# RetNet and SwiGLU in one kernel: the first pair of heads by chunks of 128 tokens behind identity products, and another order of the first loads

## The chip, the cores and the metric

The kernel runs on one core of a Trainium2 chip. The metric is device time in microseconds; lower is better. Before the change three runs took 1016.43, 1018.75 and 1019.09 us (median 1018.75). A profiled execution took 1014.55 us.

## What is computed

A retention layer feeds a gated feed-forward block. q, k and v are (8, 8, 576, 64) in float32: 8 sequences, 8 heads, 576 tokens, 64 channels.

```python
gamma = 1.0 - 2.0 ** (-5.0 - np.arange(H))                     # one decay per head
Dmat = np.where(rel >= 0, gamma[:, None, None] ** rel, 0.0)    # rel = i - j
ret = (scale * q @ k.T) * Dmat
x = (ret @ v).transpose(0, 2, 1, 3).reshape(4608, 512)
g = x @ w_gate                                                 # (512, 1536)
out = (g * sigmoid(g) * (x @ w_val)) @ w_out                   # (1536, 512)
```

The three weights arrive as float64 and are turned into float32 on the chip.

## The kernel before

**Pairs.** Two heads lie side by side on the 128 partitions and are called a pair; there are 32 of them, four per sequence. Retention is done by chunks of tokens: inside a chunk, scores times decay times v ("own values"); from earlier chunks, a running state of 64 x 64 per head ("earlier values"). Chunks have 64 tokens. For each pair, `transposes` (L448) turns k and q by products with the identity `ident` and copies them out of PSUM, `scores` (L562) makes the products of k and q, `new_states` (L537) those of k and v, `masked` (L576) multiplies scores by the decay and runs the states forward on DVE, `own_values` (L524) and `earlier_values` (L546) add up the outputs in the PSUM tile `outer`, and `to_x` (L613) copies them to the x of the next stage. Keys are scaled on ACT, DVE or, for pairs 2 and 3, on POOL (L505); for pairs 1 to 3 of the first sequence, q is scaled by position on POOL (`scale_run`, L730).

**Feed-forward.** The first 512 tokens go through plain products: `up0(f, chunks)` (L842) multiplies x by gate and value columns f of 12, where "chunks" are pairs 0 to 3 as the four pieces of the contraction. `up0(f)` writes gate and value into bankA and bankB for even f, bankC and bankE for odd f, and ends with SiLU on ACT (L856) and a product on DVE (L857). The later tokens go through tiles of 1024 with sums of operands; that part is the bulk of the run and the change leaves it alone.

**Weights.** A block of weights is 1 MB of float64. `load_w(m)` (L359) asks for the m-th block, `split(j)` (L380) takes the j-th half block apart with two ACT operations (L389, L390), `rounding(j)` (L399) puts it together with two on DVE (L406, L407) and, if `ahead` is set, calls the next `split`. Blocks 0 and 1 are gate and value of `up0(0)` and `up0(1)`, 2 and 3 of `up0(2)` and `up0(3)`, 4 and 5 of the next two. There are three landing places; block 3 has one of its own in `x_odd`. A place is free when its split is done, and `split` then asks for the next block.

**Order.** The order on each engine is the order in which the Python code issues instructions. Before, a loop over `tick(t, 0, HP)` (L737) runs the first four pairs as a pipeline: at step t, scores and states of pair t-1, own values of pair t-2, transposes of pair t, earlier values of pair t-2. Weights are first needed at step 4, when `up0(0, range(2))` (L757) is issued. Then `up0` for pieces 2 and 3 follows, and a written plan of `up0`, `rounding` and later ticks.

**Loads.** DMAs of SyncE (SP) and of ACT go out in program order, and each uses one of eight landing semaphores in turn: an issue waits until the DMA eight before has landed. SP asks for the small table (64 columns, L311), pairs 0 to 2, the big table (512 columns, L337), pair 3, the first halves of blocks 0 and 1 in pieces of 256 KB, their second halves, blocks 2 and 3 in four pieces each, pair 4 (`load(HP)`) and block 4. ACT shares the loads of pairs 0 and 1 and asks for the blocks from 5 on.

Of the kernel before, what the change touches and what calls it, by code (L numbers as in the profile page):

```python
# [22 lines left out]
def tables(gamma, scale, L):  # L23

    g, at = np.array(gamma), np.arange(L)
    lane = np.arange(2 * L)[:, None]
    both = lambda t: np.repeat(t, L, axis=0).reshape(-1, 2 * L, t.shape[1]).transpose(1, 0, 2).reshape(2 * L, -1)
    twice = lambda t: np.concatenate([t, t])
    half = [np.repeat(g.reshape(-1, 2), L, axis=1).T ** (lane % 32 + 32 * r) for r in range(2)]
    pieces = scale * np.stack(half, axis=2).reshape(2 * L, -1)
    runs = scale * (g[None, :, None] ** ((4 * lane[:, :, None] + np.arange(4)) % L)).reshape(2 * L, -1)
    parts = [twice((g[:, None] ** -at).T), twice((g[:, None] ** (L - at)).T),
             both(g[:, None] ** L), both(g[:, None] ** (2 * L)), pieces, runs, both(scale * g[:, None] ** at),
             both((scale * g[:, None] ** at).reshape(-1, 2, L)[:, ::-1].reshape(-1, L))]  # L40
    return np.concatenate(parts, axis=1).astype(np.float32)
# [90 lines left out]
def kernel(  # L132
# [32 lines left out]
    nc = tc.nc  # L165
# [88 lines left out]
    def load(i):  # L254
# [6 lines left out]
        if i < HP:  # L261
# [11 lines left out]
            for h in heads:  # L273
                queues[i % 2].dma_start(out=blocks(t)[:, h % 2], in_=v[b, h, 0:CW].rearrange("(c p) d -> p c d", p=P))
# [35 lines left out]
    NCOL = 6 * H + 4 * HP  # L310
    nc.sync.dma_start(out=tab[:, 0:NCOL], in_=decays[:, 0:NCOL])  # L311
    load(0)
    load(1)
    ident = const.tile([P, P], F32, name="ident")
    make_identity(nc, ident)
    nc.scalar.activation(out=io[:, 0:1], in_=ident[:, 0:1], func=AF.Silu)
    inv, key = tab[:, 0:H], tab[:, H : 2 * H]
    step = tab[:, 2 * H : 2 * H + 2 * HP]
    piece = tab[:, 2 * H + 2 * HP : 2 * H + 4 * HP]
    run = tab[:, 2 * H + 4 * HP : NCOL]  # L320
# [11 lines left out]
    even_heads, odd_heads = slice(0, H, 2), slice(1, H, 2)  # L332
    for rows in half:
        decay(slice(0, H), slice(0, H), rows)

    load(2)
    nc.sync.dma_start(out=tab[:, NCOL:], in_=decays[:, NCOL:])  # L337
    load(3)
# [20 lines left out]
    def load_w(m, parts=range(2)):  # L359

        i, queue = order[m], nc.sync if m < 5 else nc.scalar
        n = m - (m > RAWS)
        raw = rest[:, raw_at + n % RAWS * 2048 : raw_at + (n % RAWS + 1) * 2048].rearrange("p (c x) -> p c x", c=HP)
        if m == RAWS:
            raw = x_odd[:, :, TW // 2 :]
        raws[i] = raw.bitcast(I32)
        dst, src = raw.bitcast(I64), weights[i][0]
        if i < NUP:
            for cols in [ts(2 * f + n, D) for f in parts for n in range(2)] if m <= RAWS else [slice(0, 2 * P)]:
                queue.dma_start(out=dst[:, :, cols], in_=src[:, :, cols])  # L370
        else:
            queue.dma_start(out=dst.rearrange("p (f c) n -> p f (c n)", f=2), in_=src)
# [38 lines left out]
    for f in range(2):  # L411
        for m in range(2):
            load_w(m, (f,))
# [30 lines left out]
    def vector(i):  # L444

        return i == 0

    def transposes(i):  # L448
# [6 lines left out]
        copy = nc.scalar.copy if i else nc.vector.tensor_copy  # L455
        if i < HP:

            mine = (bankC, bankE) if i + 1 == HP else (bankB, bankA)
            parts = [(kT, kn, mine[0]), (qT, qk, mine[1])]
            if i == 0:  # L460
                parts.reverse()

            def turn(t, src, bank):
                for c in range(NFULL):
                    to = bank[:, c : 4 * P : NFULL] if t is qT and scaled(i) else bank[:, ts(c, P)]
                    nc.tensor.transpose(to, src[:, ts(c, P)], ident)

            def put(t, _, bank):
                if i or t is qT:
                    copy(t[:, 0:CW], bank)  # L470
                else:
                    copy(t[:, 0 : CW // 2], bank[:, 0 : CW // 2])
                    nc.scalar.copy(t[:, CW // 2 : CW], bank[:, CW // 2 :])

            if i + 1 == HP:
                for part in parts:
                    turn(*part)
                pieces = [lambda part=part: put(*part) for part in parts]
            else:
                for part in parts:  # L480
                    turn(*part)
                    put(*part)
# [13 lines left out]
        def keys():  # L496
# [5 lines left out]
            for hl, rows, at in parts:  # L502
                scale = key[rows, 2 * p + hl : 2 * p + hl + 1]
                if vector(i) or 1 < i < HP:
                    (nc.vector if vector(i) else nc.gpsimd).tensor_scalar(out=at, in0=at, scalar1=scale, scalar2=None, op0=ALU.mult)  # L505
                else:
                    nc.scalar.activation(out=at, in_=at, func=AF.Copy, scale=scale)
# [3 lines left out]
        return [keys] + pieces  # L511
# [64 lines left out]
    def masked(i):  # L576
# [6 lines left out]
        def copies():  # L583
            (nc.vector.tensor_copy if vector(i + 1) else nc.scalar.copy)(out=even, in_=z[:, 0])
# [151 lines left out]

    def tick(t, lo=HP, hi=NP, spread=False, then=None):  # L737
        go_on(len(pieces))
        if hi == HP:

            def new_pair():
                scores(t - 1, True)
                new_states(t - 1)
                pieces.extend(masked(t - 1))
                go_on(3)

            scale_run(t + 1)
            if lo < t < hi:
                new_pair()
            if lo <= t - 2 < hi:  # L750
                own_values(t - 2)
            for f in transposes(t) if lo <= t < hi and t + 1 < HP else ():
                f()
            if lo <= t - 2 < hi:
                earlier_values(t - 2)
                if t == HP:
                    up0(0, range(2))  # L757
                to_x(t - 2)[0]()
            if t + 1 == HP:
                split(0)  # L760
                after = transposes(t)
                rounding(0)
                for f in after:
                    f()
            if t == HP:
                rounding(2)
                rounding(3, False)
                new_pair()
                while held:
                    held.pop()()  # L770
                split(4)
                up0(1, range(2))
            return
# [68 lines left out]
    def up0(f, chunks):  # L842

        pair = banks[2 * (f % 2) : 2 * (f % 2) + 2]
        for gv, bank in enumerate(pair):
# [581 lines left out]
    for t in range(HP + 2):  # L1427
        tick(t, 0, HP)

        if t == 3:  # L1430
            load(HP)
        for j in {3: (1,), 5: (4, 5)}.get(t, ()):
            rounding(j)
    for c in range(2, HP):
        for f in range(2):
            up0(f, [c])
    load(HP + 1)
# [20 lines left out]
    plan.insert(1, lambda: tick(HP, HP, FIRST))  # L1458
    tick_at = {2: 4, 3: 5, 5: 6, 7: 7, 10: 8, 11: 9}
    for f in range(2, NF):  # L1460
        round_until({4: 12, 6: 13, 8: 14, 9: 15, 10: 16, 11: 17}.get(f, f + 2))
# [108 lines left out]
```

## Time and profile before

| | us |
|---|---|
| profiled execution | 1014.55 |
| its span on the core | 1012.8 |
| PE busy | 1000.9 |
| DVE busy | 710.9 |
| POOL busy | 561.8 |
| ACT busy | 286.7 |
| first transposes on PE (L466) | at 4.63 |
| first product with a weight (L853) | at 24.11 |
| first product of `up0(2)` (L850) | at 40.95 |

The span is the time between the first and the last instruction of the core in the profile; 1.75 us of the execution lie around it. A busy time is the union of the engine's instructions, and a matmul's record holds some 0.2 us of its passage through the array, so that neighbours overlap; the distance from start to start tells the rate. A float32 product is two passes, and counts in the profile ("x32") are passes; a transpose is one. A line of the timeline holds start, length, engine, line, operation, output <- inputs, partitions x elements, and the count; in brackets stand the idle time ahead and what ended it.

### The profile page before, as it was taken

What the parts mean: (1) busy time and instruction counts of PE and PEld (TensorE: products, weight loads), DVE (VectorE), ACT (ScalarE), POOL (GpSimd) and SP (SyncE); (2) the same over time, 40 slices, a digit from 0 to 9 for tenths busy, and PEclk for the clock granted to TensorE, in tenths of its full rate; (3) what the DMA queues carried; (4) which work ended last, traced back from release to release, by engine and by line L of the source; (5) the groups of instructions that cost most, each with busy time, mean ns of one, the idle gap of its engine ahead of it and who ended that gap; (6) DMA issues with size and microseconds to landing.
All of it is one profiled execution on the core that took longest, in us unless ns stands there. A gap on an engine that the chain in (4) does not pass through costs nothing.

```text
span 1012.8 us, 21319 instructions
## 1 busy us (share of the span) xinstructions
PE 1000.9 (99%) x8336; PEld 825.5 (82%) x8336; DVE 710.9 (70%) x1206; ACT 286.7 (28%) x636; POOL 561.8 (55%) x589
## 2 busy tenths in 40 slices
PE   6999999999999999999999999999999999999998
PEld 5655555888888888888888888888888888888887
DVE  4488887677875766977777678866575767566645
ACT  4565522132423312133422202233220012232110
POOL 3400359979375228575564157746672586566514
PEclk9999999999999999999999999999999999999999
DMA  9999866967587787647677777434454554445553
GB/s 245 261 288 272 192 216 234 264 193 214 138 238 207 217 231 193 198 156 196 184 202 206 198 179 217 154 133 159 161 172 141 154 189 147 148 155 180 182 159 102
DMA packets 278892, 194.38 MB, mean 192 GB/s; under 512 B 212552, under 2 KB 246088, under 8 KB 278792
## 3 DMA queue, kind: packets, MB, share of 16 engines
q1 hardware_dynamic: 251464, 94.70, 36.7%
q10 hardware_dynamic: 26688, 97.92, 29.1%
q8 instruction: 66, 1.08, 0.5%
q0 software_dynamic: 640, 0.39, 0.2%
q14 instruction: 34, 0.28, 0.1%
HBM read 154.04 MB, written 38.93 MB: 191 GB/s over the span
## 4 chain that ended last, share of the span: by engine, by line
PE 94%; DVE 2%; DMA 1%; POOL 1%; SPq 0%; issue 0%; ACT 0%; DVEq 0%; ACTq 0%; POOLq 0%
PE bankB L1186 12%; PE bankC L1186 11%; PE bankA L1186 11%; PE bankE L1186 11%; PE bankB L1392 7%; PE bankC L1392 7%; PE bankE L1392 6%; PE bankA L1392 6%; PE outer L532 2%; PE bankE L853 2%; PE bankA L853 2%; PE outer L1186 2%; PE inner L1186 2%; PE bankB L853 2%; PE outer L559 2%; PE bankC L853 2%
## 5 line engine op out<-in xcount | busy, mean ns | idle before, releaser
L1042 POOL TENSOR_TENSOR rest<-rest 128x512 f32<-128x512 f32 (+1 forms) x139 | 148.0, 1076 | 159.9 <-DVE rest L1042 112.5
L1201 POOL TENSOR_TENSOR arena<-rest,io 128x256 f32<-128x256 f32 x168 | 123.9, 750 | 89.4 <-ACT io L1200 88.9
L1200 ACT ACTIVATE io<-rest 128x256 f32<-128x256 f32 x192 | 79.3, 417 | 200.0 <-DVE rest L1042 140.0
L1186 PE MATMUL bankB<-rest,arena 128*128 128x256 f32 x448 | 114.5, 380 | 0.0
L1042 DVE TENSOR_TENSOR rest<-bankB,rest 128x512 f32<-128x512 f32 x116 | 78.5, 685 | 40.5 <-PE bankB L1186 28.5
L1186 PE MATMUL bankC<-rest,arena 128*128 128x256 f32 x416 | 106.3, 380 | 0.0
L1186 PE MATMUL bankA<-rest,arena 128*128 128x256 f32 x412 | 104.8, 379 | 0.0
L1042 DVE TENSOR_TENSOR rest<-bankA,rest 128x512 f32<-128x512 f32 x111 | 75.2, 685 | 40.8 <-PE bankA L1186 19.3
L1042 DVE TENSOR_TENSOR rest<-bankC,rest 128x512 f32<-128x512 f32 x110 | 74.5, 683 | 38.0 <-PE bankC L1186 23.4
L1042 DVE TENSOR_TENSOR rest<-bankE,rest 128x512 f32<-128x512 f32 x106 | 71.7, 684 | 36.2 <-PE bankE L1186 17.6
L1186 PE MATMUL bankE<-rest,arena 128*128 128x256 f32 x372 | 94.9, 380 | 0.3 <-DVE rest L1042 0.3
L1186 PEld LDWEIGHTS bankB<-rest,arena 128*128 128x128 f32 x448 | 84.7, 190 | 11.9 <-DVE rest L1042 0.2
L1186 PEld LDWEIGHTS bankC<-rest,arena 128*128 128x128 f32 x416 | 78.5, 190 | 11.4 <-DVE rest L1042 0.8
L1186 PEld LDWEIGHTS bankA<-rest,arena 128*128 128x128 f32 x412 | 78.1, 190 | 10.9 <-DVE rest L1042 0.2
L1186 PEld LDWEIGHTS bankE<-rest,arena 128*128 128x128 f32 x372 | 70.3, 190 | 10.4 <-DVE rest L1042 0.8
L1042 POOL TENSOR_TENSOR arena<-arena 128x256 f32<-128x256 f32 (+1 forms) x76 | 70.3, 947 | 11.1 <-PE bankC L1186 9.0
L886 POOL TENSOR_TENSOR rest<-rest 128x512 f32<-128x512 f32 x21 | 28.5, 1377 | 72.1 <-DVE rest L407 58.5
L1392 PE MATMUL bankB<-arena 128*128 128x256 f32 x264 | 61.0, 381 | 0.0
L1392 PE MATMUL bankE<-arena 128*128 128x256 f32 x264 | 60.8, 380 | 0.0
L1392 PEld LDWEIGHTS bankE<-arena 128*128 128x128 f32 x264 | 50.0, 190 | 6.9
L1392 PEld LDWEIGHTS bankB<-arena 128*128 128x128 f32 x264 | 49.8, 190 | 6.9
L1392 PE MATMUL bankC<-arena 128*128 128x256 f32 x240 | 55.2, 379 | 0.0
(270 smaller groups left out, 1876.0 us busy)
## 6 DMA issues: line engine op xcount, KB each, us to landing
arena<-up ACTq DMA_DIRECT2D x63, 896.0 KB, 4.6
arena<-dn ACTq DMA_DIRECT2D x65, 384.0 KB, 3.1
arena<-dn SPq DMA_DIRECT2D x39, 384.0 KB, 3.1
out_dram<-rest SPq DMA_DIRECT2D x31, 256.0 KB, 3.4
qk<-in_q_dram SPq DMA_DIRECT2D x108, 72.0 KB, 3.1
qk<-in_k_dram SPq DMA_DIRECT2D x108, 72.0 KB, 3.4
dn<-rest SPq DMA_DIRECT2D x26, 256.0 KB, 2.8
up<-arena SPq DMA_DIRECT2D x13, 512.0 KB, 5.6
```

What stands on the lines that cost most here:

```text
L532: m = nc.tensor.matmul(value(i, hl, c), s["v"][rows, at], ret[rows, c % 2 if whole(i) else hl, c // 2], start=start, stop=start, skip_grou ...
L559: nc.tensor.matmul(xr[half[hl]] if c + 1 == NC else value(i, hl, c), state[half[hl], c, :], s["qT"][half[hl], ts(c, L)], start=False, stop ...
L853: nc.tensor.matmul(bank, w, xs[0][:, c, :], start=(c == 0), stop=(c == HP - 1))
L886: eng.tensor_tensor(out=dst, in0=srcs[0], in1=srcs[1], op=ALU.add if op[0] == "add" else ALU.subtract)
L1042: eng.tensor_tensor(out=out, in0=a, in1=b, op=ALU.add if sign > 0 else ALU.subtract)
L1186: m = nc.tensor.matmul(b[:, g * TB : (g + 1) * TB], w[:, g], x, start=(opens and g == 0), stop=True, skip_group_check=True)
L1200: nc.scalar.activation(out=s, in_=src[:, 0:TB], func=AF.Silu)
L1201: (nc.vector if busy and o != 2 and qd + 1 < NQ else nc.gpsimd).tensor_tensor(out=hid[:, qd, 2 * H + h, 2 * T + t], in0=src[:, TB : 2 * TB ...
L1392: nc.tensor.matmul(b[:, m * TB : (m + 1) * TB], lhs[:, qd, ts(m, P)], w[:, qd], start=(opens and qd == 0 and m == 0), stop=(qd == NQ - 1), ...
```

## The change

It has four parts.

1. **Pair 0 by chunks of 128 tokens.** `first_scores`, `first_states`, `first_own` and `first_out` replace the general functions for pair 0: 8 products of 128 x 128 for scores instead of 16 of 64 x 64, 8 for the states, 8 for own values, 6 for earlier ones. q is scaled where it is copied out of PSUM, so the output is a plain ACT copy. Three small tables (4 + 128 columns) are added to the first table.
2. **Identity products.** `first_scores` begins with two 64 x 64 and six 128 x 128 products of the identity with itself, and has two and one more behind the transposes of q and k. Six small ones also stand ahead of the first up product.
3. **The order of the first stage is written out.** The first product of `up0(0)` now stands behind own values of pair 1, and the further ones between the work of pairs 1 to 3.
4. **Loads.** SP asks for q and k of pair 0 first, then the table. The values of a pair are a step of their own (`values`). The first halves of blocks 0 and 1 come ahead of pair 3, their second halves behind it; blocks 2 and 3 are one DMA each. Block 4 now stands ahead of pair 4, the big table behind it. Block 5 is asked for on ACT behind the outputs of pair 3 (`held`), and `split(6)` behind `up0` of all four pieces. `tick(HP, HP, FIRST)` moves from ahead of `up0(2)` to behind it.

```diff
-    NCOL = 6 * H + 4 * HP
-    nc.sync.dma_start(out=tab[:, 0:NCOL], in_=decays[:, 0:NCOL])
-    load(0)
-    load(1)
+    NCOL = 6 * H + 4 * HP + 4 + P
+    values = [load(0), load(1)]
     ident = const.tile([P, P], F32, name="ident")
     make_identity(nc, ident)
     nc.scalar.activation(out=io[:, 0:1], in_=ident[:, 0:1], func=AF.Silu)
+    for f in values:
+        f()
+    load(2)()
...
-    load(2)
-    nc.sync.dma_start(out=tab[:, NCOL:], in_=decays[:, NCOL:])
-    load(3)
...
-            for cols in [ts(2 * f + n, D) for f in parts for n in range(2)] if m <= RAWS else [slice(0, 2 * P)]:
+            for cols in [ts(2 * f + n, D) for f in parts for n in range(2)] if m < 2 else [slice(0, 2 * P)]:
...
-    for f in range(2):
-        for m in range(2):
-            load_w(m, (f,))
+    for m in range(2):
+        load_w(m, (0,))
+    load(3)()
+    for m in range(2):
+        load_w(m, (1,))
     load_w(2)
     load_w(3)
...
+    def first_scores():
...
+        for _ in range(2):
+            nc.tensor.matmul(bankB[0:D, 0:D], ident[0:D, 0:D], ident[0:D, 0:D], start=True, stop=True)
+        for src, bank, idle in ((None, None, 6), (qk, bankE, 2), (kn, bankC, 1)):
+            for c in range(NFULL if bank else 0):
+                nc.tensor.transpose(bank[:, ts(c, P)], src[:, ts(c, P)], ident)
+            for _ in range(idle):
+                nc.tensor.matmul(bankB[:, 0:P], ident, ident, start=True, stop=True)
...
+        nc.vector.tensor_tensor(out=blocks(qT), in0=blocks(bankE), in1=table(first_qry), op=ALU.mult)
+        nc.vector.tensor_copy(kT[:, 0 : CW // 2], bankC[:, 0 : CW // 2])
+        nc.scalar.copy(kT[:, CW // 2 : CW], bankC[:, CW // 2 :])
+        for hl in range(2):
+            at = kn[:, 0:CW].rearrange("p (g d) -> p g d", d=D)[:, hl::2]
+            nc.vector.tensor_scalar(out=at, in0=at, scalar1=first_key[:, hl : hl + 1], scalar2=None, op0=ALU.mult)
+        for c, hl in first:
+            nc.tensor.matmul(inner[:, hl, ts(c, P)], kT[half[hl], ts(c, P)], qT[half[hl], ts(c, P)],
+                             start=True, stop=True, skip_group_check=True)
+        for hl in range(2):
+            nc.vector.tensor_tensor(out=first_ret[:, hl], in0=blocks(inner[:, hl]), in1=table(first_near[:, ts(hl, P)]), op=ALU.mult)
+
+    def first_states():
...
+    def first_own():
...
+    def first_out():
...
-    for t in range(HP + 2):
-        tick(t, 0, HP)
-
-        if t == 3:
-            load(HP)
-        for j in {3: (1,), 5: (4, 5)}.get(t, ()):
-            rounding(j)
+    scale_run(1)
+    first_scores()
+    scale_run(2)
+    turn_pair(1)
+    first_states()
+    first_own()
+    new_pair(1)
+    turn_pair(2)
+    first_out()
+    split(0)
+    rounding(0, False)
+    scale_run(3)
+    new_pair(2)
+    own_values(1)
+    split(1)
+    for _ in range(6):
+        nc.tensor.matmul(bankB[0:D, 0:D], ident[0:D, 0:D], ident[0:D, 0:D], start=True, stop=True)
+    up0(0, [0], [0])
+    earlier_values(1)
+    to_x(1)[0]()
+    put = transposes(3)
+    rounding(1, False)
+    for f in put:
+        f()
+    up0(0, [1], [0])
+    up0(0, [0], [1])
+    split(2)
+    own_values(2)
+    earlier_values(2)
+    up0(0, [1], [1])
+    to_x(2)[0]()
+    rounding(2)
+    rounding(3, False)
+    new_pair(3)
+    load(HP)
+    nc.sync.dma_start(out=tab[:, NCOL:], in_=decays[:, NCOL:])
+    split(4)
+    up0(1, range(2))
+    own_values(3)
+    earlier_values(3)
+    to_x(3)[0]()
+    while held:
+        held.pop()()
+    rounding(4)
+    rounding(5, False)
     for c in range(2, HP):
         for f in range(2):
             up0(f, [c])
+    split(6)
     load(HP + 1)
...
     round_until(3)
-    plan.insert(1, lambda: tick(HP, HP, FIRST))
     tick_at = {2: 4, 3: 5, 5: 6, 7: 7, 10: 8, 11: 9}
     for f in range(2, NF):
+        if f == 3:
+            plan.append(lambda: tick(HP, HP, FIRST))
```

## The prediction, written before the changed kernel ran

> **What bounds the kernel now.** I read the windows first: they tell whether TensorE ever has slack. Columns: stretch in us, its length, busy us and instructions of PE, PE weight loads, DVE, ACT and POOL, the granted clock, the DMA share, GB/s.
>
> ```profile
> 0.00:10.00 10.00, 4.50 (x74) 3.57 (x75) 1.64 (x4) 2.18 (x4) 3.21 (x11) 1.00 0.96 203
> 10.00:20.00 10.00, 9.03 (x240) 7.77 (x241) 6.57 (x16) 3.94 (x9) 3.96 (x4) 1.00 1.20 269
> 20.00:30.00 10.00, 8.83 (x171) 5.61 (x172) 7.21 (x16) 8.15 (x17) 1.97 (x2) 1.00 1.06 287
> 30.00:40.00 10.00, 9.82 (x80) 4.68 (x80) 4.67 (x11) 5.34 (x10) 8.30 (x16) 1.00 1.03 247
> 40.00:50.00 10.00, 10.00 (x45) 8.36 (x44) 4.27 (x9) 3.40 (x7) 4.22 (x8) 1.00 1.13 268
> ```
>
> From 34 us to the end TensorE has work all the time; what the change can win lies before that, where the DMA engines are full too. The waits of PE say the same: over the whole span, these are all above 0.25 us:
>
> ```profile
> PE bankA L466 <- DMA qk<-in_q_dram: 4.6, 1, 4.6
> PE outer L532 <- ACT rest L389: 1.0, 1, 1.0
> PE inner L573 <- ACT rest L470: 0.7, 1, 0.7
> PE inner L573 <- DVE kT L472: 0.5, 1, 0.5
> PE bankB L466 <- DMA kn<-in_k_dram: 0.3, 1, 0.3
> PE bankE L1186 <- DVE rest L1042: 0.3, 1, 0.3
> ```
>
> The timeline then shows that PE's first 17 us are slow as well as broken. The same four transposes, and the same 32 passes of scores, before and after 17 us:
>
> ```profile
> 12.36 1.13 PE L573 MATMUL inner<-rest,kT 64*64 64x64 f32 x32 [0.72 <-ACT rest L470]
> ...
> 16.03 1.06 PE L466 MATMUL bankA<-ident,rest 128*128 128x128 f32 x4
> ...
> 21.03 0.60 PE L466 MATMUL bankE<-ident,rest 128*128 128x128 f32 x4
> ...
> 24.11 1.98 PE L853 MATMUL bankA<-rest,arena 128*128 128x512 f32 x4
> ...
> 27.74 0.69 PE L573 MATMUL inner<-rest,kT 64*64 64x64 f32 x32
> ...
> 40.95 3.62 PE L850 MATMUL bankA<-rest,arena 128*128 128x256 f32 x16
> ```
>
> Start to start a transpose takes 0.213 us up to 17.0 us and 0.109 from there on, though the clock column says 1.00 throughout; I call this cold and warm. Two lines are my milestones: 24.11, the first up product, and 40.95, where `up0(2)` begins. Behind 40.95 PE's order is the same in both kernels (the moved `tick(HP)` has no matmul), so **the gain is how much earlier `up0(2)` starts**, less any new wait behind it.
>
> **Part 1, PE's work up to `up0(2)`.** Before, 24.11 to 40.95 is 16.84 us: 32 passes of 128x512 at 0.43 (13.7), scores and states of pair 3 (27.74 to 28.86: 1.12), own and earlier values of pair 3 (32.49 to 33.98: 1.49), and 0.5 at changes of shape. The change puts the first up product (one matmul, two passes) in front of work that stood before 24.11. Behind it now come also earlier values of pair 1 (19.93 to 20.54: 0.61), transposes of pair 3 (eight at 0.11 plus 0.05: 0.93), own and earlier values of pair 2 (1.45), and three more changes of shape at about 0.2 (the next group starts at 25.93, 1.82 after 24.11 where four passes are 1.72, and the first one came 0.14 late). Sum: 16.84 + 0.61 + 0.93 + 1.45 + 0.6 = **20.4 us** from the first up product to `up0(2)`.
>
> **Part 2, when the first up product can start.** It needs the first half of weight 0 in bits: landing, two ACT passes (L389 and L390: 0.57 to the second's start, 0.65), one DVE pass (L407: 0.69). Landings I read from the trace's landing marks (last of sixteen per DMA). Before, the four pieces of w0 and w1, first halves, land at 18.87, 19.76, 20.60 and 21.41, pair 3 ahead of them. Steps between landings: a q 0.42, a k 0.6, a v 0.57, a weight piece 0.85, the big table 0.69. The change puts pair 3 behind these halves (2 x (0.42 + 0.6 + 0.57) = 3.2), and the big table behind `load(HP)` (0.69); it widens the first table from 64 to 196 columns (68 KB, about 0.2). So w1's half lands at 21.41 - 3.2 - 0.7 + 0.2 = 17.7 and w0's at 16.0. Then 16.0 + 0.57 + 0.65 + 0.1 + 0.69 = 18.0, **PE at 18.1**.
>
> Is PE there by then? q and k of pair 0 stand first in both queues now and land at about 4.1 and 5.4 (before 4.50 and 5.88). Identity products 1.6 to 4.3 (six of two passes at 0.21); transposes of q to 5.2, two identity products, of k 6.0 to 6.9; copies of kT on DVE and ACT to 7.9. If the clock is warm by then, scores (eight 128x128 products, 0.21 each) end at 9.4, transposes of pair 1 at 10.3, ACT's two copies and two key scalings (0.59 and 0.45 each) at 12.2, states of pair 1 at 13.0, transposes of pair 2 at 14.0, `first_out` 14.7. Keys of pair 2 on POOL (L505, 1.87 for two) run 13.8 to 15.7, its states to 16.3, own values of pair 1 to 17.0. So PE waits about 1 us for the weight.
>
> The products of 128 tokens appear in no row. Eight scores are at least 1.14 us (the 32 small passes they replace, cold) and at most 3.4 (16 cold passes at 0.21); I take 1.7, as for transposes at the warm rate. Own values and outputs of pair 0 (28 passes of 128 columns on half the array) lie between 1.5 (two at a time) and 3.0; I take 1.5, because 64x64 passes on separate parts of the array start 7 ns apart here. The higher ends add 1.5 and reach the first up product by 0.5 at most, since 1 us of waiting covers them. The saving below the low ends is nothing, as the weight decides.
>
> **Part 3, waits behind 18.1.** Earlier values of pair 1 end at 19.7; pair 3's k lands at 17.7 + 0.84 + 1.2 = 19.8, so its transposes wait 0.1; ACT copies pair 1's x (L640, 1.13) by 21.0 behind `split(1)`, and PE waits 0.3 for it. Later ones I find covered: `rounding(1)` ends at 21.8 for a product at 22.0, `rounding(3)` at 27.6 for one at 28.2. Sum: 18.1 + 20.4 + 0.4 = 38.9, **2.1 us before 40.95**.
>
> **Part 4, loads.** w2 and w3 are one DMA each, not four. The 2 KB rows have a row: w6, 1 MB, lands 2.95 us behind its predecessor, against 4 x 0.85; I count 2.9. Then w2 lands at 27.3 (before 28.70), w3 30.2, w4 33 (before 49.19, since SP's queue had `load(HP)` ahead). w5, asked for on ACT behind `to_x(3)` at 33 and not 29.64, lands near 38 (before 36.79). Its bits were wanted at 59.57, now about 57; ACT's split of it waits in line behind w4's, so the delay costs nothing. What ACT holds up: `split(4)` stands ahead of `to_x(3)` and waits for w2, with `to_x(3)`, w5's DMA and both SiLUs queued behind it; `to_x(3)` may come as late as 35 before PE's last chunk waits. `split(6)` now comes after the second SiLU (39.0); bits at 41.0, wanted at 42.3: 1.3 us of cover. `load(HP)` lands earlier than its 45.22. The big table is wanted only around 72 us (L658).
>
> **Sum.** -2.1 us. The profiled execution is 1014.55 us (span 1012.8 and 1.75 around it), so about 1012.4 by its own account; the three times shown have a median 4.2 above it, and on that median, 1018.75, it is 1016.65. I say **1016.6**.
>
> **A rule weighed.** Row first: before, PE had no gap from 13.3 to 17.0, about half of it transposes (15.12 to 17.0), and the rate doubled at 17.0. The Trainium skill, "TensorE: Matmul & The Clock Gate", Part 4, says that transposes do not count as busy for the clock gate; the row speaks against that. By that rule the stretch 4.3 to 7.2, mostly transposes, would not warm the clock: rival C.
>
> **Rivals.**
> - B, no lag. From 16 to 30 us the last mark of each DMA trails its first by 2 us, where it was 0.6 up to then; if the halves of w0 come without that, at 15, ACT is free at 15.5, PE starts at 17.4 and then waits for ACT's x of pair 1 (20.6). `up0(2)` at 38.1: -2.9, 1015.9. For it: bytes come to 3 MB by 14.7 at the rate seen. Against: the trail began as soon as weight pieces were in flight.
> - C, identity products do not warm the clock: it doubles only after the scores, at 11 or later. For it: 7.6 to 11.6 before, with gaps of 17%, stayed cold. Scores end 1.7 later, transposes of pair 1 cost 0.9 more, own values 0.5: PE reaches 20 us, 1.9 behind 18.1 less what later waits forgive (0.4): -0.6, 1018.1.
> - D, slower: the weight becomes the bound. PE's order puts the up product, hence w0's landing, ahead of earlier(1), transposes(3) and all the rest, where before nothing of PE waited for a weight before 24. Each us of landing past 16.0 costs one. Up to 18.1 that eats the gain; from there it is a loss. Landing at 20.6, as the third piece does before, gives +2.5, and 21.4, as the fourth, +3.3; I put the case at +2.8, 1021.5. For it: these pieces showed the lag, and each trails what is in flight. Against: the big table and six DMAs of 128 KB no longer stand ahead of them.
>
> **How the numbers follow.** A 47%, B 25%, C 17%, D 11%. The four times known of this kernel, the profiled one among them, spread over 4.5 us, and 0.3% (3.06 us) is about what a measurement here can tell. Faster by more: half of B and two fifths of A, 0.32; slower by more: three fifths of D, 0.07; within: 0.61. Range: down to PE's own floor (first up product at 17.1, behind own values of pair 1: -3.1) less half that spread, 1013.3; up to C plus half of it, 1020.4. Only most of D is left out.
>
> **What would show it.** In the changed profile: passes of scores at about 0.1 us start to start by 8 us (A, B) or 0.21 (C); first up product at 18.1 behind a wait on DVE's rounding (A), 17.4 (B), 20 without a wait (C) or with one (D); `up0(2)` at 38.9; no PE wait above 0.3 us behind it. A wait at `up0(2)`'s bankB would mean `split(6)` had too little cover, and would make the prediction wrong.

## The result: slower by 0.56%

The changed kernel took 1023.39 us (median of 8 runs, 1020.11 to 1024.44); the kernel before took 1017.09 us beside it (8 runs, 1015.59 to 1019.09). The ratio is 1.0056, with a 95% interval of 1.0040 to 1.0071. The forecast was 1016.6 us, from 1013.3 to 1020.4, so both its sign and its range were wrong.

The profiled execution took 1021.79 us with a span of 1020.1 us, 7.3 us more than before. I matched TensorE's instructions of the two traces from their ends backwards and compared the times at which the same instruction starts. That gives TensorE's lag behind the kernel before, the most useful number here (the first column is the time in the kernel before, the stops have their times in the changed kernel):

| at, us | lag, us | what lies in between |
|---|---|---|
| 43 | -1.95 | the first stage, as forecast |
| 75 | -0.33 | a stop at 72.13 |
| 110 | +1.53 | a stop at 104.69 |
| 130 | +3.43 | a stop at 127.82 |
| 285 | +3.48 | nothing |
| 370 | +5.41 | stops at 291, 311 and 367 |
| 430 | +7.54 | stops at 415, 416 and 436 |
| end | +7.33 | nothing |

So there are three parts: 1.95 us won up to `up0(2)`, 5.4 us lost from 43 to 140 us (the lag at 140 is 3.4), and 3.9 us lost behind 140 us, where both kernels issue the same instructions in the same order.

**The first part** came out as forecast. The timeline of PE in the changed kernel has the two milestones at 18.48 (forecast 18.1) and 39.00 (forecast 38.9; before 40.95):

```profile
18.48 1.12 PE L869 MATMUL bankA<-rest,arena 128*128 128x512 f32 x2 [0.99 <-DVE arena L416]
...
39.00 3.19 PE L866 MATMUL bankA<-rest,arena 128*128 128x256 f32 x14
```

**The second part** shows in PE's waits over the span (total, times, longest). The first two lines are new and are the three stops up to 130 us; the third is the wait for `ident` at the start, and the fourth the wait for the rounding, which was forecast at 1 us:

```profile
PE bankA L869 <- ACT io L872: 3.1, 2, 1.6
PE bankE L880 <- DVE arena L873: 1.6, 1, 1.6
PE bankB L732 <- POOL ident masks.py:199: 1.6, 1, 1.6
PE bankA L869 <- DVE arena L416: 1.0, 1, 1.0
```

PE waits there for SiLUs and products that free its banks. ACT is busy for 28% of the span, so it is not slow; it is held up. ACT's waits from 38 to 75 us say by what:

```profile
ACT kn L492 <- DMA kn<-in_k_dram: 9.8, 1, 9.8
ACT rest L398 <- DMA qk<-in_k_dram: 5.0, 1, 5.0
```

The first is the key scaling of pair 5, whose keys landed at 64.86 us (57.31 before). The second looks absurd: a split of a weight waits for keys. ACT's timeline explains it:

```profile
43.16 0.68 ACT L399 ACTIVATE rest<-rest 128x512 int32<-128x512 uint32 x1
48.32 0.37 ACTq L381 DMA_DIRECT2D rest<-in_moe_w_out_dram  x1
48.79 0.68 ACT L398 ACTIVATE rest<-rest 128x512 f32<-128x512 f32 x1 [4.95 <-DMA qk<-in_k_dram]
49.37 0.67 ACT L399 ACTIVATE rest<-rest 128x512 int32<-128x512 uint32 x1
49.92 0.61 ACT L872 ACTIVATE io<-bankA 128x512 f32<-128x512 f32 x1
```

ACT stands at the issue of a DMA (L381). That DMA uses one of the eight landing semaphores, and the last user of the same one was a k of pair 4, issued at 36.00 and landed at 48.24. Each DMA here sets sixteen landing marks; fifteen of this one's came by 42.99, and the last alone at 48.24. The issue follows 0.08 us later, and the SiLU of `up0(2)` behind it in line. All of pair 4 is late: its last k landed at 48.68 (42.33 before), its kn at 49.58 (43.91 before).

**The third part** has stops whose releaser the profile gives as "issue", that is, none. This is the one at 367 us, in PE's timeline:

```profile
364.59 0.63 PE L558 MATMUL inner<-qT,kT 64*64 64x64 f32 x30
365.16 1.99 PE L1408 MATMUL bankB<-arena 128*128 128x256 f32 x8
367.52 1.13 PE L1408 MATMUL bankB<-arena 128*128 128x256 f32 x4 [0.37 <-issue]
```

PE stops 0.53 us beyond its usual pitch in the middle of one group of twelve passes, with all operands at hand.

### The profile page after: what moved, and what is told of

Its sections match the earlier page's. It is cut to its first block, busy times and chain, and to the rows that moved or that the text cites. A ratio compares the mean times of both kernels' runs of the same rounds, so it can differ in the third digit from the quotient of the medians.

```text
span 1020.1 us, 21247 instructions
## 1 busy us (share of the span) xinstructions
PE 1005.0 (99%) x8306; PEld 828.0 (81%) x8306; DVE 713.7 (70%) x1203; ACT 285.9 (28%) x636; POOL 561.6 (55%) x590
## 4 chain that ended last, share of the span: by engine, by line
PE 85%; DMA 5%; DVE 3%; ACT 2%; SPq 2%; POOL 1%; issue 1%; ACTq 0%; DVEq 0%; POOLq 0%
PE bankB L1202 11%; PE bankC L1202 11%; PE bankA L1202 11%; PE bankE L1202 11%; PE bankB L1408 7%; PE bankC L1408 7%; PE bankE L1408 6%; PE bankA L1408 6%; PE outer L1202 2%; PE inner L1202 2%; PE outer L517 2%; PE outer L544 1%; DMA rest<-in_moe_w_gate_dram 1%; POOL rest L1058 1%; DMA qk<-in_q_dram 1%; PE inner L558 1%
```

## The experiments

My theories for the 43 to 140 us part were at first Q (block 4 ahead of pair 4 on SP's queue), M (`tick(HP)` moved behind `up0(2)`) and W (w2 and w3 as one DMA each). Others came as these fell. The ratio is to the kernel before, with its 95% interval; the lags are of one profiled execution each, which scatter by some us, so verdicts go by the ratio.

| kernel | ratio | lag at 43 | at 140 | at the end |
|---|---|---|---|---|
| changed | 1.0056 (1.0040 to 1.0071) | -2.0 | 3.4 | 7.3 |
| e1_pair_first | 1.0050 (1.0036 to 1.0064) | -2.2 | 4.6 | 5.3 |
| e2_tick_back | 1.0028 (1.0016 to 1.0040) | -2.4 | 0.2 | 1.8 |
| e3_pieces | 1.0066 (1.0049 to 1.0082) | -0.5 | 4.9 | 9.2 |
| e4_pair_and_tick | 1.0033 (1.0018 to 1.0047) | -1.9 | 2.6 | 5.0 |
| e6_both_and_sixth | 1.0035 (1.0022 to 1.0048) | 0.5 | 5.4 | 9.5 |
| e7_tick_and_sixth | 1.0027 (1.0015 to 1.0040) | -0.3 | 3.0 | 6.4 |
| e8_before_sixth_late | 0.9998 (0.9985 to 1.0011) | 1.2 | 1.2 | 1.2 |
| e9_before_tick_late | 1.0012 (1.0000 to 1.0025) | 0.8 | 4.5 | 5.0 |
| x1_first_stage_only | 1.0048 (1.0031 to 1.0066) | -2.0 | 4.9 | 5.5 |
| x2_first_stage_and_table | 1.0043 (1.0028 to 1.0058) | -1.5 | 1.8 | 4.5 |
| x3_pool_asks | 1.0033 (1.0016 to 1.0049) | -2.1 | 2.2 | 4.3 |
| x5_before_pool_asks | 0.9992 (0.9982 to 1.0002) | 0.3 | 0.3 | 0.2 |
| y4_pair3_ahead | 1.0067 (1.0044 to 1.0090) | 3.6 | 5.4 | 6.8 |
| y1_wide_halves | 1.0029 (1.0011 to 1.0048) | -2.8 | 2.2 | 5.5 |
| y2_wide_tick_pool | 1.0025 (1.0012 to 1.0037) | -2.7 | -0.7 | 2.9 |
| e5_no_ident | 1019.33 us, one run | -1.0 | 1.9 | 4.9 |
| z1_code_shift | 1.0038 (1.0026 to 1.0050) | -1.8 | 4.1 | 4.1 |
| z2_all_repairs | 1.0016 (1.0002 to 1.0030) | 1.0 | 3.7 | 3.8 |

**e1_pair_first.** `load(HP)` ahead of the fifth block.

```diff
+    load(HP)
     split(2)
     own_values(2)
```

> Pair 4's loads (`load(HP)`) stand on SyncE's queue ahead of `split(2)`, so ahead of the fifth weight block, and not behind it; nothing else differs from the changed kernel. Theory Q (order of the queue): in the changed kernel the 1 MB block in front of pair 4 makes pair 4's k land at 48 us and not at 42, ScalarE's 4.95 us stop and the late key scalings follow, and three stops of TensorE (72.1, 104.7, 127.8 us: 5.3 us together). Then here k of pair 4 lands by 43.5, the three stops are below 0.5 us each, the span falls from 1020.1 to 1014 to 1016, and the ratio to the kernel before is 0.997 to 1.001. Theory M (the moved `tick(HP)`: transposes of pair 4 later on VectorE, hence pair 5 later): pair 4 lands early, but VectorE still turns it only behind the third SiLU, and the stops at 104.7 and 127.8 stay: span 1018 to 1020, ratio 1.003 to 1.006. Theory W (w2 and w3 asked for as one DMA each): as M, no change.

Pair 4's last k landed at 41.87 and the three old stops were gone, as Q says, but the ratio stayed at 1.0050. In their place PE stopped 3.6 us at 56 for pair 4's keys, which ACT scaled only behind the fifth block (landed at 51.03). Q by itself falls: the order on the queue only chooses who is late.

**e2_tick_back.** `tick(HP)` ahead of `up0(2)` again.

```diff
     round_until(3)
+    plan.insert(1, lambda: tick(HP, HP, FIRST))
```

> `tick(HP)` stands again as second entry of the plan, ahead of `up0(2)`, as before the change; the loads stay as changed. Theory Q: pair 4's k still lands at 48 us, so VectorE, whose transposes of pair 4 now stand earlier in its line, waits for it in front of the roundings: TensorE's stops stay or grow, span 1020 to 1024, ratio 1.005 to 1.010. Theory M: VectorE turns pair 4 by 50, pair 5 lands some us earlier than its 66.5, the stops at 104.7 and 127.8 vanish: span 1015 to 1017, ratio 0.999 to 1.002.

The ratio fell to 1.0028, half of the loss, with kn of pair 5 at 62.15 (64.86 in the changed kernel). M holds for a part: it had promised 0.999 to 1.002, and of the two stops that were to vanish, one of 1.3 us is left (124.59).

**e3_pieces.** w2 and w3 in four pieces each.

```diff
-... for n in range(2)] if m < 2 else [slice(0, 2 * P)]:
+... for n in range(2)] if m <= RAWS else [slice(0, 2 * P)]:
```

> Blocks w2 and w3 are asked for in four pieces each again, as before the change, not in one DMA each. Theory Q and theory M: no difference above 1 us from the changed kernel (span 1019 to 1021, ratio 1.004 to 1.007), as 4 pieces of 0.85 us and one DMA of 3.2 us take the same time. Theory W (the single large DMAs, or the landing semaphores that they share, delay what follows): pair 4's k lands 2 us or more earlier than 48 and the stops of TensorE shrink by half: ratio 1.000 to 1.003.

1.0066, not better: W falls.

**e4_pair_and_tick** is both e1 and e2.

> Both: pair 4 ahead of the fifth block on SyncE's queue, and `tick(HP)` as second entry of the plan, so behind `up0(1)` all is as before the change but for the big table (behind pair 4) and the sixth block (asked for behind `to_x(3)`). Theory Q: as with the queue's order alone, within 1 us. Theory M, if both it and Q hold: better than either alone, by 1 to 3 us. If the whole loss is in these two, the time is that of the kernel before less the 2 us won up to `up0(2)`: span 1011, ratio 0.997 to 0.999. If more is lost than that, the rest lies with the big table, the sixth block or behind 290 us.

1.0033: as e2 alone. More than these two is at work.

**e6_both_and_sixth, e7_tick_and_sixth, e8_before_sixth_late, e9_before_tick_late.** The sixth block ahead of `split(4)` again (on e4 and e2), and each suspect alone put into the kernel before.

```diff
+    while held:
+        held.pop()()
     split(4)
     up0(1, range(2))
```

> As e4 (pair 4 ahead of the fifth block, `tick(HP)` as second entry of the plan), and the sixth block w5 is asked for ahead of `split(4)`, as before the change, and not behind `to_x(3)`. Theory S (the late sixth block): in e4 nothing large is under way on the DMA engines from 30 to 35 us (103 GB/s, 283 before the change), since w5 is issued at 33.73 where it was 29.64; what follows lands some 4 us later for its place. By S w5 lands by 37.5, the first kn of pair 4 by 44 (45.98 in e4), w4 by 49 (50.89), TensorE's stops at 55.7, 103.5 and 124 are below 0.5 us each, and the ratio to the kernel before is 0.997 to 1.000 (1.0033 in e4). If w5's place is of no account, the ratio stays 1.002 to 1.005.

> As e2 (`tick(HP)` as second entry of the plan, SyncE's order as changed: fifth block ahead of pair 4), and the sixth block asked for ahead of `split(4)`. If the fifth block's place ahead of pair 4 costs nothing once the other two are undone, the ratio is as in e6, 0.997 to 1.000. If it costs by itself (pair 4's k landed at 47 in e2), the ratio is 1.001 to 1.004 and ScalarE's wait for the slot of that k's landing semaphore (5.0 us in the changed kernel) is there again.

> The kernel before, with one thing of the change alone: the sixth block is asked for behind `to_x(3)` (at about 35.2 us, not 29.64). Theory S: the DMA engines' rate falls below 200 GB/s between 30 and 36 us, kn of pair 4 lands 2 us or more later than 43.91, w4 later than 50.5, and the ratio is 1.001 to 1.004. By the prediction on record (its delay costs nothing): 0.999 to 1.001.

> The kernel before, with one thing of the change alone: `tick(HP)` (keys and transposes of pair 4) stands behind `up0(2)` in the plan. Theory M (its place costs by itself): VectorE turns pair 4 at about 50 us and not 42.9, pair 5 lands 3 us or more later than its 61.63, TensorE stops for 1 us or more between 70 and 130, ratio 1.002 to 1.004. If its place costs only where the loads are late: ratio 0.999 to 1.001.

Theory S falls: e6 is 1.0035 and e7 1.0027, as e4 and e2 were, and e8 is level with the kernel before. The forecast that this delay costs nothing was right. e8's lag of 1.2 us is there from 43 us on and comes from the first stage. e9 is 1.0012, between its two forecasts, and the interval reaches 1.0000: whether the tick's place costs by itself is not shown.

**x1_first_stage_only, x2_first_stage_and_table.** All undone behind the first stage; x2 leaves the big table behind pair 4.

> The changed first stage (pair 0 by 128 tokens, identity products, pair 3 behind the first halves of w0 and w1, the order of TensorE's products up to `up0(2)`), and all the rest of the change undone: w2 and w3 in four pieces, pair 4 ahead of the fifth block, the sixth block ahead of `split(4)`, `split(6)` ahead of the outputs of `up0(0)` and `up0(1)`, `tick(HP)` second in the plan, and the big table asked for right behind pair 3. Theory R (the loss lies in one or several of these later parts): the 2 us won at `up0(2)` reach the end: ratio 0.996 to 0.999. Theory F (the first stage itself brings it: TensorE is 2 us ahead, the loads are not, and what it gains it waits for, or the loads of pair 3 in front of the later blocks delay all that follows): ratio 1.001 to 1.004, with stops of TensorE behind 41 us as in e6.

> As x1, but the big table behind pair 4 on SyncE's queue, as in the changed kernel. Theory T (the table's place costs: 0.7 us of transfer and one more landing semaphore in the middle of the loads of pairs 4 and 5): 0.001 to 0.003 above x1. Otherwise within 0.001 of it.

1.0048 and 1.0043: theory R falls, T falls, F stands, though its range (1.001 to 1.004) was too low. The first stage alone, 2.0 us earlier at `up0(2)`, ends up as slow. In x1 PE's timeline has one large stop, where the SiLU of `up0(2)` stands on ACT behind the splits of the fifth block, which landed at 53.13 (49.19 before):

```profile
53.43 0.64 PE L559 MATMUL inner<-qT,kT 64*64 64x64 f32 x30
57.86 6.63 PE L870 MATMUL bankA<-rest,arena 128*128 128x512 f32 x8 [3.79 <-ACT io L873]
64.33 3.60 PE L870 MATMUL bankB<-rest,arena 128*128 128x512 f32 x8
```

From the group behind the stop to the next it is 6.47 us; such a group of eight passes takes 3.4 at full rate. So the stop of 4.0 us costs some 7. The last section comes back to that.

**x3_pool_asks, x5_before_pool_asks.** The blocks from the sixth on asked for by GpSimd, whose DMAs have other landing semaphores, in the changed kernel and in the one before.

```diff
-        i, queue = order[m], nc.sync if m < 5 else nc.scalar
+        i, queue = order[m], nc.sync if m < 5 else nc.gpsimd
```

> The changed kernel, with the weight blocks from the sixth on asked for by GpSimd and not by ScalarE; GpSimd's DMAs have landing semaphores of their own (111 to 118), and ScalarE holds up nothing for a free one. Theory L (landing semaphores: in the changed kernel three of ScalarE's DMA issues, at 37.41, 48.32 and 73.88 us, come 0.07 to 0.08 us behind the landing of an unrelated transfer that had the same one of the eight, with ScalarE stopped ahead of them, 4.95 us at 43.8 above all; in the kernel before only one does, at 29.64): TensorE's stops at 72, 104 and 128 us shrink to below half (5.3 us in the changed kernel), ratio 0.998 to 1.002. If the late transfers themselves are the cause, not ScalarE's waits for a slot: ratio 1.004 to 1.007 as before.

> The kernel before, with the weight blocks from the sixth on asked for by GpSimd. It is the control for x3: if the change of queue by itself neither wins nor loses, ratio 0.998 to 1.002; GpSimd's line may hold up a block behind its own work (its keys of pairs 2 and 3, its decay tables), which would show as a later issue than 36.38 us for the seventh block and a ratio above 1.002.

x3 is 1.0033, between the two expectations; its profile has no stop at 72 or 104 and one of 2.5 us at 125. x5 is level with the kernel before, so the queue as such is free. ACT's waits for a landing semaphore are likely a part of the loss; the intervals of x3 and of the changed kernel overlap (1.0040 to 1.0049).

**y4_pair3_ahead, y1_wide_halves, y2_wide_tick_pool, e5_no_ident.** The loads of the first stage in the old order (on x1); the halves of w0 and w1, and q of pair 3, as fewer and larger DMAs; this with e2's and x3's edits; the changed kernel without the nine identity products of 128 columns.

```diff
-[ts(2 * f + n, D) for f in parts for n in range(2)] if m < 2
+[ts(f, 2 * D) for f in parts] if m < 2
```

> As x1, with pair 3 and the big table asked for ahead of the first halves of w0 and w1 again, so that the loads stand in the order of the kernel before; TensorE's order stays the changed one. Theory D (loads of the first stage: with pair 3 behind the halves the DMA engines run half empty from 18 to 20 us, 0.27 MB there in x1 and 0.57 before, all later loads land late, w4 at 53.1 in x1 and 49.2 before, and TensorE stops for it): the rate from 15 to 20 us is above 260 GB/s, w4 lands by 50.5, the first up product comes at about 21 to 22 us and `up0(2)` near 41, no stop above 1 us behind it, ratio 0.999 to 1.002 (1.0048 in x1). Theory E (TensorE's order itself): w4 lands as late as in x1 and the ratio is 1.004 to 1.006.

> The changed kernel, with each half of w0 and w1 as one DMA of 0.5 MB and not two of 0.26 MB, and q of pair 3 as one DMA and not two. Five landing semaphores fewer are taken from 10 to 21 us, so more bytes can be under way in the eight that there are. If the hole of 15 to 20 us (200 GB/s) comes from the eight semaphores being held by small transfers, it fills to above 245 GB/s, pair 4's k lands 1 us or more earlier than 48.2, and the ratio falls by 0.001 to 0.003 from 1.0056. If not, rate and ratio stay.

> The three repairs together on the changed kernel: wide halves (y1), `tick(HP)` second in the plan (e2: 0.0028 less than the changed kernel's 0.0056), weight blocks from the sixth on asked for by GpSimd (x3: 0.0023 less). If they add, the ratio is 0.997 to 1.001 and TensorE's 2 us of `up0(2)` reach the end; if they mend the same waits, 1.001 to 1.003.

> The changed kernel without its nine identity products of 128 columns in the first stage (six ahead of q's transposes, two behind them, one behind k's). If the products themselves warm the clock and transposes do not count (the Trainium skill, 'TensorE: Matmul & The Clock Gate', Part 4, states the latter), the scores of pair 0 and the transposes of pairs 1 and 2 run at 0.21 us start to start up to 11 us or later. If transposes count as work, as the row of the kernel before suggests (rate doubled at 17.0 after a stretch half of transposes), the rate doubles some 2 to 3 us later than the 6.4 us of the changed kernel, but still by 10 us. Either way the first up product stays within 0.5 us of 18.5, since it waits for the weight.

y4 is 1.0067 with the rate of the DMA engines from 15 to 20 us back at 265 GB/s: theory D falls as the whole cause. E, which gave w4 as late as 53.1 and 1.004 to 1.006, is not met either: w4 landed at 51.90. The first up product came at 22.59, which is rival D of the prediction, and `up0(2)` at 44.56, 3.6 us late. But PE lost only 1.8 us from 43 to 140, where x1 lost 6.9. A lead that is given back is a part of the loss, but not all of it: e6 is 0.5 us behind at 43 and loses 4.8 more.

y1 is 1.0029: larger transfers from 10 to 21 us seem to help (the intervals overlap from 1.0040 to 1.0048). Pair 4's last k landed at 46.09, but the rate from 15 to 20 us only rose from 200 to 230 GB/s, not above 245. y2 is 1.0025, no better than its best part; three repairs of 0.0023 to 0.0028 do not add, as if they mended the same waits.

In e5 scores and the first transposes behind them run cold, and the rate doubles at 10.4 us, in the middle of transposes (at 6.9 in the changed kernel). That is between the two forecasts, 11 us or later and by 10. The scores of pair 0 start at 6.79 here; nothing but scores and transposes runs from there to the doubling:

```profile
6.79 1.23 PE L747 MATMUL inner<-rest,kT 64*128 64x128 f32 x8 [0.86 <-DVE kT L741]
8.19 1.22 PE L747 MATMUL inner<-rest,kT 64*128 64x128 f32 x8 [0.18 <-ACT kT L742]
9.35 1.11 PE L466 MATMUL bankC<-ident,kn 128*128 128x128 f32 x4
10.26 0.68 PE L466 MATMUL bankE<-ident,qk 128*128 128x128 f32 x4
```

The first up product came at 19.42, not within 0.5 of 18.5, because of a stop of 1.6 us at 18.18 with no releaser.

**z1_code_shift, z2_all_repairs.** Every stop of 0.3 us or more that the profile gives no releaser, some 40 in all runs together, apart from passes at half rate, starts at one of two places modulo 256 in the count of PE's instructions: 193 or 194. The page lists PE's own instruction queue among the DMA queues (packets, MB, share): 66 packets of 16 KB. Over PE's 16,900 instructions that is 64 bytes for each, so 256 to a packet.

```profile
q8 instruction: 66, 1.08, 0.5%
```

The changed first stage has 63 PE instructions fewer (16,894 records, 16,957 before). So each block of the instruction stream begins 63 instructions later in the work. At the stop of 367 us the packet starts at 365.14, takes 0.93, and PE goes on at 367.52; at 291 and 311 too, PE goes on 2.3 to 2.4 us behind the start of a packet.

The kernel before pays as well, in its first stage. This line of its PE timeline is at place 194, 2.56 us behind the start of a packet (20.06), though the profile puts the wait down to an ACT split, which is not among the operands; the same instruction waits 1.8 us in x5 and 2.1 in e8:

```profile
22.62 0.69 PE L532 MATMUL outer<-ret,v 64*64 64x64 f32 x32 [0.99 <-ACT rest L389]
```

z1 adds 16 small identity products, that is 64 instructions, where PE has little else to do.

```diff
-    for _ in range(6):
+    for _ in range(16):
         nc.tensor.matmul(bankB[0:D, 0:D], ident[0:D, 0:D], ident[0:D, 0:D], start=True, stop=True)
```

Six more stand in `first_scores` (two at its start, four behind k's transposes).

> The changed kernel with 16 more identity products of 64x64 (64 instructions of TensorE: 8 at the start, 16 behind k's transposes, 40 where TensorE waits 1 us for the first rounding), whose output nobody reads. They put the block boundaries of TensorE's instruction stream within 1 instruction of where they fall in the kernel before. Theory B (blocks): the stops without a releaser behind 140 us (0.73, 0.50 and 0.53 us at 291, 311 and 367 in the changed kernel) vanish, the drift of TensorE against the kernel before behind 140 us falls from 3.9 to below 1.5 us, and the ratio from 1.0056 to 1.002 to 1.004; the stops of 40 to 130 us stay. If the stops there have another cause, they stay, and the ratio is 1.005 to 1.007 (the products may cost up to 0.3 us at the first up product).

> y2 (wide halves, `tick(HP)` second in the plan, blocks from the sixth on asked for by GpSimd) with the same 16 products. In y2's profile TensorE is 0.66 us ahead of the kernel before at 285 us and 2.89 behind at the end, 1.2 of it in a stop without a releaser at 362 and up to 1.6 at 749. Theory B: these go, the drift behind 140 us is below 1.5 us, ratio 0.998 to 1.001, so the change with its four repairs is at least level with the kernel before. Otherwise as y2: 1.0015 to 1.0035.

Theory B holds. In z1 the lag is 4.1 us at 140 and 4.1 at the end, where the changed kernel goes from 3.4 to 7.3; the stops of that stretch are gone, those put down to DVE at 415, 416 and 436 too but for 0.3 us at 414. How the blocks would bring those of DVE, some 2 us in all, is not shown. PE's timeline of z1 at the place of the 367 us stop has the group in one piece:

```profile
364.00 0.63 PE L558 MATMUL inner<-qT,kT 64*64 64x64 f32 x30
364.56 2.86 PE L1410 MATMUL bankB<-arena 128*128 128x256 f32 x12
367.26 2.75 PE L1410 MATMUL bankE<-arena 128*128 128x256 f32 x12
```

The ratio fell from 1.0056 to 1.0038, as expected, but the intervals overlap (1.0040 to 1.0050), so the lags are the stronger evidence. Those of all runs agree: from 140 us to the end, the 14 kernels whose blocks lie elsewhere lose 0.6 to 4.3 us (mean 2.7), and the five whose blocks lie as in the kernel before, to a few instructions, (e8, e9, x5, z1, z2) between -0.1 and 0.5.

z2 is 1.0016 (1.0002 to 1.0030), the best of the kernels with the new first stage and still not faster than the kernel before. From 140 us to the end it loses 0.1 us, as theory B says, but the ratio lies in the range of the other case (1.0015 to 1.0035). Its profile shows the same effect inside the first stage, where the shift did not move it out of harm's way. PE stops 2.1 us in the states of pair 2, at place 194 of a block:

```profile
15.45 0.52 PE L532 MATMUL inner<-v,rest 64*64 64x64 f32 x3
17.76 0.63 PE L532 MATMUL inner<-v,rest 64*64 64x64 f32 x27 [1.79 <-issue]
```

## Why the prediction was wrong

**Right.** Part 2 (PE at 18.1): 18.48; w0's first half landed at 16.37 for 16.0. Parts 1 and 3 gave 20.4 us of work and 0.4 of waits from there to `up0(2)`: together 20.52. So 39.00 for 38.9 is in part luck: a start 0.4 us late and a stretch 0.3 short nearly cancel. The rate doubled at 6.9 us and scores took 1.32 us, so rival C is out. D did not happen either; y4, where w0's half landed at 20.49, shows that its price was low (3.6 us where the prediction had 2.5 for 20.6): from the first up product to `up0(2)` it took 21.97 us, with the granted clock at 0.50 from 22.6 to 26.8. In Part 4, w5's delay costs nothing (e8).

B is out in the changed kernel: the fifteenth mark of w0's second piece came at 14.90, the last at 16.37. In e1 and x2 w0's half landed without that trail, at 14.76 and 14.83, and the first up product still came at 18.23 and 18.26, not at B's 17.4: PE stopped 0.9 us at place 194 (16.69 and 16.72). The trail goes with PE's first instruction packet: of the twelve kernels that load w0's half in two pieces ahead of pair 3, the nine with that packet at 12.80 to 13.67 us have it, the three with it at 14.08 or later do not. No run moved the packet alone to test this.

**The step that failed** is the one that carried the sum from `up0(2)` to the end: "Behind 40.95 PE's order is the same in both kernels [...], so the gain is how much earlier `up0(2)` starts, less any new wait behind it", with "no PE wait above 0.3 us behind it". Two things broke it.

First, "`load(HP)` lands earlier than its 45.22": its last value landed at 50.73, 5.5 us later. I had put the loads in a line and counted their bytes; w2, w3, w4 and w5 landed at 28.64, 31.82, 35.91 and 41.86 for 27.3, 30.2, 33 and 38. The runs show more than a line: the issue of each DMA waits for a landing semaphore that some other transfer holds, ACT stands in line at such issues (x3: 0.0023), and larger transfers in the eight semaphores gain 0.0027 (y1). The loads of 30 to 65 us then land later than before, and PE stops three times from 72 to 128 us (5.3 us), at banks that ACT and VectorE free late. Moving `tick(HP)` I had dismissed because it has no matmul, but undoing it wins 0.0028 (e2), the clearest gain of a single repair: VectorE then turns pair 4 from 42 to 49 us and not from 51 to 53, and pair 5's keys land 2.7 us earlier. What links the two, the traces do not show.

This part is not wholly settled. x1 and y4 undo the order of nearly all loads and still lose as much as the changed kernel, and the repairs do not add. Which property of the first stage makes the loads of 30 to 55 us land late in x1 (the fifth block 3.9 us later, from the same place in the line) stays open. One profiled execution per kernel is little evidence on landings: in e9 the same block landed at 51.29, with the same DMAs ahead of it as in the kernel before.

Second, 3.9 us behind 140 us came with a thing that the prediction did not have at all: the places where PE's instruction blocks begin. z1 and the lags of the other kernels show it. The Trainium skill, "Runtime: NRT & Kernel Launch", section "Instruction fetch mechanics", has the blocks of 16 KiB with 256 instructions, and says that the cost of crossing a boundary is "mostly hidden". The trace agrees on the blocks; on the cost, most of the 66 crossings show none, and the ones here cost 0.3 to 2.2 us. The stops at 291, 311 and 367 lie in or just behind runs of 64x64 passes (30 in 0.57 us in the lines above), which, with a weight load each, use up a block of 256 in some 2.4 us (an estimate from that pitch).

## What to carry to other kernels

An engine that gets ahead gains only if its operands do: before summing what an engine saves, list what each later wait ends on, and move the loads in the sum as well, with the semaphores and in-order engines through which they are asked for. Taking instructions away shifts the instruction stream for all work behind them; where a kernel runs near its bound, compare the lag of the same instruction in both traces from end to end, and look at stops without a releaser by their place in the stream. A few harmless instructions that put the stream back, as in z1, separate this effect from the change itself.

## What the runs showed that I had not expected

**Half the clock behind a stop.** In x1 the granted clock, the third column from the right in the windows, is halved for 6 us behind the stop of 4.0 us:

```profile
54.00:57.80 3.80, 0.07 (x5) 0.00 (x0) 2.10 (x4) 3.29 (x7) 0.00 (x0) 0.89 0.81 155
57.80:61.00 3.20, 3.14 (x4) 1.51 (x5) 2.75 (x5) 2.69 (x6) 0.00 (x0) 0.50 1.01 366
61.00:64.00 3.00, 3.00 (x5) 1.11 (x4) 2.66 (x8) 2.39 (x6) 0.00 (x0) 0.54 1.08 359
64.00:67.00 3.00, 3.00 (x9) 1.33 (x8) 2.96 (x8) 0.05 (x1) 0.00 (x0) 1.00 1.15 240
```

Passes there take 0.85 us from start to start and 0.43 from 64 us on, which is how the stop of 4.0 us costs some 7. The same came with stops of 5.5 us (y4), 3.6 (e1), 3.15 (y1), 2.5 (x3) and 2.34 (e3), but with shorter ones too: 1.7 us in e9 (at 17.87), two with 0.6 and 0.5 us of idle time in e9 (at 56 and 58), and 1.8 in e5, a stop at an instruction block:

```profile
620.23 0.45 PE L558 MATMUL inner<-qT,kT 64*64 64x64 f32 x12 [1.63 <-issue]
...
621.40:624.80 3.40, 3.40 (x10) 2.65 (x9) 2.69 (x6) 0.56 (x2) 0.37 (x1) 0.50 0.51 173
624.80:628.00 3.20, 3.20 (x16) 2.83 (x15) 2.64 (x5) 0.00 (x0) 0.00 (x0) 1.00 0.02 5
```

Behind others of 2.34 to 2.64 us (z1, e6, z2) the clock stayed at 1.00, so the length of the stop alone does not decide. In these traces the granted clock changes in steps of 3.41 us: it is halved for one (e3, e5, e9, x3, y1) or two (e1, x1, y4). e3 and z1 stop for the same 2.34 us; in e3 the stop lies within one step (104.10 to 107.51), in z1 a step ends in it, at 105.36. That fits, but was not tested. The Trainium skill, "TensorE: Matmul & The Clock Gate", section "Why this matters for your kernels", warns of idle gaps above some 3 us; here shorter ones did it, down to 1.7 us and less.

**Transposes and the clock.** The rate doubles where a trace's clock records begin (17.15 us before, 6.89 in the changed kernel); the column's 1.00 ahead of that stands for no record, not for full speed. The first stage of the kernel before got there at 17.15 us, in e8 at 16.13, in x5 at 15.71 and in e9 at 11.30, so one row says little about rival C. In e5 scores fill 63% of the 3.41 us ahead of the doubling, so it does not decide whether transposes count. Two other traces say more: in the kernel before, the step ahead of the doubling (13.74 to 17.15) holds 1.97 us of transposes and 1.4 of products; in e4 the step from 0.96 to 4.37 holds 2.82 us of products and no transpose, and the rate stayed low up to 7.78. That speaks against the rule that the prediction weighed, that transposes do not count; a case with transposes alone was not run.
